# A recurrent memory transformer's forward step, joined differently: V's projection behind the scores, heads paired by parity, V's rows moved by GpSimd, DMA and VectorE

## The chip, the cores and the metric

One Trainium2 chip, one core of it. The time is the device time of the whole kernel in microseconds (us); runs of the kernel before lie between 3055.53 and 3083.94, median 3065.29 (3 runs). Profiles are single executions; all durations below are from the profiled execution of the kernel before.

Engines: TensorE (PE; PEld is its weight load), VectorE (DVE), ScalarE (ACT), GpSimd (POOL) and SyncE (SP, which here only issues DMAs). Each engine and each issuing queue works in the order in which its instructions were written.

## The reference

A pre-norm block: attention over segments with a recurrent memory, then a SwiGLU feed-forward, and the gradients of all weights and inputs for a given output gradient. What matters here is the attention, with 2048 tokens of width 448, 16 heads of width 256, 64 segments of 32 tokens and 8 memory rows, so L = 40 rows a segment:

```python
for s in range(n_seg):
    xs = x[:, s * seg_len:(s + 1) * seg_len, :].copy()
    h = jnp.concatenate([mem, xs], axis=1)
    q = jnp.einsum('btd,dhe->bhte', h, Wq)
    k = jnp.einsum('btd,dhe->bhte', h, Wk)
    v = jnp.einsum('btd,dhe->bhte', h, Wv)
    scores = jnp.einsum('bhqe,bhke->bhqk', q, k) * scale
    scores = jnp.where(mask[None, None], scores, -1000000000.0)
    p = _softmax(scores, axis=-1)
    o = jnp.einsum('bhqk,bhke->bhqe', p, v)
    o = jnp.einsum('bhte,hed->btd', o, Wo)
    mem = o[:, :M, :].copy()
    outs.append(o[:, M:, :])
```

The memory of segment s+1 is an output of segment s, so the 64 steps can't overlap except for work on rows that don't depend on the memory. The gradient runs through the same 64 steps backwards.

## The kernel before

Four stages run one after the other: the forward loop over 64 segments (`forward_chain`), the feed-forward with its gradients, the backward loop over 64 segments (`backward_chain`), and the weight gradients. The order of every engine's instructions is that of the source (a manual schedule): nothing is reordered.

*Rows.* A segment has 40 rows: the 8 memory rows and the first 24 tokens (32 rows, "A", that need the memory or stand beside it) and the last 8 tokens ("B"). B rows of four segments are projected together, a tile of four segments ahead, in pieces used as filler in the steps (`b_units`, L530: `u1` 16 matmuls, `u2` and `u3` 8 each; every fourth step `o_units`, L586, instead).

*Projections.* `proj` (L464) makes half the columns of one projection, for four groups of 1024 columns (four heads each): 16 matmuls of 512 columns, group g written to the PSUM rows 32g to 32g+31. So a half has two heads of each group, and token t of group g stands in row 32g+t.

*A forward step* (loop at L671), in the order of TensorE: K both halves, V first half, Q first half, turned half of K (`tr_half`, L474, four transposes), Q second half, turned halves of K and Q, V second half in two pieces around the last turned half of Q, scores in two halves of 16 matmuls (L505), 24 filler matmuls, two and one dummy matmuls of 512 columns (`spin`, L847), the turn of P's first half (8 transposes of 40x40, L761), masks for the next step (L488), the turn of the second half, 8 filler matmuls, PV (32 matmuls of 40 rows by 40 columns, L792), output projection (64 matmuls of 224 columns, L583), two transposes of the summed result (L513). A VectorE sum (L518) writes the memory rows of the next step, and that starts its projections.

*V's rows.* PV needs V with a segment's 40 rows as the contraction: `V_sb`, groups 0 and 1 in rows 0 to 39, groups 2 and 3 in rows 64 to 103. The evacuated projection `Vev` has the groups in rows 32g instead, so V's rows are moved (`v_shift`, L649): four pieces of 32 rows by 512 columns a half. Before, VectorE moves the first half's four pieces ahead of the scores, GpSimd two pieces of the second half, and VectorE the last two after the turned P. The 8 B rows come by four small DMAs on SP (`v_b_rows`, L641) that wait until the step before has used V_sb. SP then also stores V (two DMAs, L777), K (L706) and Q (L719) for the backward loop, and GpSimd's queue stores P (L774).

*Softmax.* On VectorE and ScalarE, in two halves (L738 to L748). P is written as `P_sb[104, 8 heads, 40]`: heads 0 to 7 in rows 0 to 39, heads 8 to 15 in rows 64 to 103. The turned P (`PT`) is copied out of PSUM once by VectorE and once by ScalarE.

*A backward step* (loop in `backward_chain`) projects the output's gradient (L1173), evacuates it (`dOev`), turns it (`doT`, L1179) for the scores' gradient (L1452), and moves its rows into `dO_sb` as V's above: `shift`, with the two pieces (0, 1) of the second half on ScalarE behind its copy of `doT`. It loads P (`load_P`) and turned V (`load_vT`) a step or more ahead.

## Time and profile before

| | us |
|---|---|
| median of 3 runs | 3065.29 |
| the profiled execution's own time | 3067.6 |
| its span (first to last instruction) | 3065.8 |
| first 58.8 of the span | loads and first tile |
| 58.8 to 1038 | forward loop, 64 steps |
| 1038 to 1400 | feed-forward |
| 1400 to 2375 | backward loop, 64 steps |
| 2375 to 3065.8 | weight gradients |
| TensorE busy, forward loop | 928.48 of 979.20 |
| VectorE busy, forward loop | 587.00 of 979.20 |
| ScalarE busy, forward loop | 445.66 of 979.20 |

How to read it: the page gives busy time by engine, the chain of work that ended last, and groups of instructions by line. The chain is followed back from the last instruction, at each step to what released it; "issue" is time in which an engine waited for nothing that the profile shows. A line of the chain has its start, its length, the engine, the tile that it wrote and the source line, often that of a helper: L431 is a VectorE copy and L434 a ScalarE copy of the forward loop, L1164 and L1167 those of the backward loop. A TensorE entry that looks busy may be pipelined. In a line of the timeline the number after the start is the time from the first instruction of a merged group to its last one's end.

### The profile page before, as it was taken

To read this page: it belongs to the slowest core of one execution; us is meant where nothing else is said; L and a number is where in the kernel's file an instruction comes from. 1 tells how busy PE (TensorE), PEld (TensorE's weight loads), DVE (VectorE), ACT (ScalarE), POOL (GpSimd) and SP (SyncE) were. 2 spreads that over 40 slices of the span, in tenths; PEclk is the share of its full clock that TensorE was granted. 3 is DMA by queue.
4 is the path that set the end of the run, shared out by engine and by line. 5 is a ranking of instruction groups with operands and counts; after the bars stand their busy time and mean duration, and the time that the engine had idled before them with its cause. 6 is when DMAs were issued, how large, how long until landed. Compare 5 with 4: busy or idle time off the path is not lost.

```text
span 3065.8 us, 108383 instructions
## 1 busy us (share of the span) xinstructions
PE 2825.9 (92%) x46532; PEld 1540.9 (50%) x46568; DVE 1546.5 (50%) x4123; ACT 1175.4 (38%) x3023; POOL 738.1 (24%) x1384
## 2 busy tenths in 40 slices
PE   3999999999999699995999999999998999989999
PEld 1555555555555355552555555555554454444454
DVE  4566666666655477772655566556554112211221
ACT  2444444444444356562444444444443111101110
POOL 1222222222222122221222222223222222223332
PEclk7999999999999899997999999999999999999999
DMA  8333333333333773348566566555566999999996
GB/s 262 101 103 114 114 104 108 119 104 105 107 119 99 200 181 116 117 133 188 138 183 154 143 177 158 143 169 171 138 158 197 309 222 197 197 204 208 195 208 135
DMA packets 612448, 482.84 MB, mean 157 GB/s; under 512 B 482944, under 2 KB 526544, under 8 KB 602432
## 3 DMA queue, kind: packets, MB, share of 16 engines
q1 hardware_dynamic: 565632, 289.17, 43.6%
q0 software_dynamic: 46336, 186.74, 18.3%
q8 instruction: 366, 6.00, 0.8%
q14 instruction: 114, 0.93, 0.1%
HBM read 135.08 MB, written 219.52 MB: 116 GB/s over the span
## 4 chain that ended last, share of the span: by engine, by line
PE 75%; issue 6%; DMA 5%; DVE 5%; ACT 5%; SPq 2%; POOL 1%; POOLq 0%; ACTq 0%; DVEq 0%
PE psf L468 14%; PE psf L1669 12%; PE psf L1200 10%; PE psf L1173 4%; PE psf L583 4%; PE psf L1474 3%; PE psf L1654 3%; PE psf L978 3%; PE psh L474 3%; ACT dO_sb L1167 2%; PE psf L1682 2%; PE psf L1061 2%; DMA wall<-in_A_Wv_dram 2%; PE s_ps L847 1%; PE pob L1200 1%
## 5 line engine op out<-in xcount | busy, mean ns | idle before, releaser
L468 PE MATMUL psf<-wall,hA 112*32 112x512 bf16 x6144 | 379.3, 381 | 17.0 <-DVE hA L518 15.2
L1669 PE MATMUL psf<-wall,H_all 128*128 128x512 bf16 x1404 | 320.9, 381 | 13.1 <-DMA wall<-dKA 11.0
L1669 PEld LDWEIGHTS <-H_all 128*128 128x128 bf16 x1440 | 139.5, 98 | 178.2 <-issue 21.2
L468 PEld LDWEIGHTS <-hA 112*32 112x32 bf16 x6144 | 140.5, 96 | 163.8 <-DVE hA L518 31.3
L1581 DVE CAST resc<-psf 128x512 bf16<-128x512 f32 (+1 forms) x58 | 39.1, 673 | 317.4 <-PE psf L1669 283.3
L731 POOL COPY V_sb<-Vev 32x512 bf16<-32x512 bf16 x128 | 77.6, 606 | 341.0 <-PE s_ps L505 329.9
L1579 ACT CAST resc<-psf 128x512 bf16<-128x512 f32 (+1 forms) x54 | 31.0, 574 | 329.0 <-PE psf L1669 291.6
L1525 POOL COPY dmem<-dA 128x32 bf16<-128x32 bf16 x63 | 13.3, 211 | 553.8 <-DVE dA L1212 553.8
L468 PE MATMUL psf<-wall,hB 112*32 112x512 bf16 x1536 | 105.6, 397 | 32.8 <-DMA wall<-in_A_Wk_dram 13.4
L1164 DVE COPY partC<-psf 128x224 f32<-128x224 f32 x64 | 25.1, 392 | 219.6 <-ACT partC L1167 219.6
L1173 PE MATMUL psf<-wall,dA 128*32 128x512 bf16 x2048 | 123.4, 383 | 13.0 <-DVE dA L1212 13.0
L1654 PEld LDWEIGHTS <-wall 128*128 128x128 bf16 x864 | 84.3, 99 | 90.4 <-issue 12.6
L1654 PE MATMUL psf<-dOut_all,wall 128*128 128x448 bf16 x640 | 125.7, 355 | 3.3 <-DMA wall<-OTA 3.3
L583 PE MATMUL psf<-wall,oA 128*32 128x224 bf16 x4096 | 115.5, 268 | 11.8 <-DVE oA L431 11.6
L1200 PE MATMUL psf<-wall,dkA 128*32 128x448 bf16 x2048 | 112.0, 361 | 14.3 <-DMA wall<-in_A_Wk_dram 13.0
L1164 DVE COPY dO_sb<-dOev 32x512 bf16<-32x512 bf16 x256 | 121.0, 472 | 7.1
L1200 PE MATMUL psf<-wall,dqA 128*32 128x448 bf16 x2048 | 111.1, 357 | 13.0 <-DMA wall<-in_A_Wq_dram 10.0
L1200 PE MATMUL psf<-wall,dvA 128*32 128x448 bf16 x2048 | 121.8, 357 | 0.7 <-issue 0.7
L431 DVE COPY V_sb<-Vev 32x512 bf16<-32x512 bf16 x384 | 109.4, 285 | 9.2
L1167 ACT CAST dOev<-psf 128x512 bf16<-128x512 f32 x64 | 37.5, 586 | 184.7 <-PE psf L1173 180.9
L583 PEld LDWEIGHTS <-oA 128*32 128x32 bf16 x4096 | 97.3, 99 | 19.7 <-DVE oA L431 18.4
L1200 PE MATMUL pob<-wall 128*32 128x448 bf16 x1536 | 106.4, 356 | 0.3 <-issue 0.3
(281 smaller groups left out, 5736.2 us busy)
## 6 DMA issues: line engine op xcount, KB each, us to landing
Vtok<-V_sb SPq DMA_DIRECT2D x128, 192.0 KB
KtokA<-Kev SPq DMA_DIRECT2D x64, 256.0 KB
QtokA<-Qev SPq DMA_DIRECT2D x64, 256.0 KB
OTA<-oA POOLq DMA_DIRECT2D x16, 1024.0 KB
Q_sb<-QtokA SPq DMA_DIRECT2D x128, 128.0 KB
K_sb<-KtokA SPq DMA_DIRECT2D x128, 128.0 KB
dVA<-dvA POOLq DMA_DIRECT2D x16, 1024.0 KB
dKA<-dkA POOLq DMA_DIRECT2D x16, 1024.0 KB
```

The lines of the kernel that those rows point to most:

```text
L431: nc.vector.tensor_copy(out=out, in_=in_)
L468: nc.tensor.matmul(ps[32 * g:32 * g + 32, :], lhsT=stat(kc), rhs=W_sb[0:DB, kc, c0:c0 + HB], start=(kc == 0), stop=(kc == KC - 1))
L474: nc.tensor.transpose(pt[:, j * P:(j + 1) * P], ev[:, half * HB + j * P:half * HB + (j + 1) * P], ident[:, :])
L583: nc.tensor.matmul(ps[32 * g:32 * g + 32, 0:2 * DB], lhsT=x, rhs=Wo_sb[:, c, a * 2 * DB:(a + 1) * 2 * DB], start=first, stop=last)
L978: nc.tensor.matmul(out[b][:, 0:BW], lhsT=xT[:, kc, :], rhs=Wx[:, kc, f0:f0 + BW], start=(kc == 0), stop=False)
L1164: nc.vector.tensor_copy(out=out, in_=in_)
L1167: nc.scalar.copy(out=out, in_=in_)
L1173: nc.tensor.matmul(ps[32 * g:32 * g + 32, :], lhsT=stat(kc), rhs=WoT_sb[:, kc, c0:c0 + HB], start=(kc == 0), stop=(kc == KC - 1))
L1200: nc.tensor.matmul(pO[32 * g:32 * g + 32, 0:D], lhsT=ch(c), rhs=WT[:, c, :], start=(first and i < 4), stop=(last and i >= MC - 4), skip_gr ...
L1474: nc.tensor.matmul(po[:, n * L:(n + 1) * L], lhsT=lhs[b:b + L, lc:lc + P], rhs=rhs[b:b + L, hh, :], start=True, stop=True)
L1654: nc.tensor.matmul(ps[:, 0:D], lhsT=stat[:, i, c * P:(c + 1) * P], rhs=Y[:, i, 0:D], start=(i == 0), stop=(i == kts - 1))
L1669: nc.tensor.matmul(ps[:, 0:N], lhsT=Hx[:, i, dc * P:(dc + 1) * P], rhs=X[:, i, b * N:(b + 1) * N], start=(i == 0), stop=(i == kts - 1))
```

## The change

In the forward step, the order of TensorE is now: K, Q (both halves each), four turned halves, V first half, scores, V second half, then 16 filler matmuls, the masks, the turns of P with 8 filler matmuls between, PV's first half, 8 filler matmuls, PV's second half. The dummy matmuls are gone.

V is projected by parity of the head (`proj_v`): even heads to rows 0 to 63, odd heads to rows 64 to 127 of the result, so after the row move V_sb has even heads in rows 0 to 39 and odd heads in rows 64 to 103. P is written with 64 columns a head, so that a block of 128 columns holds two heads; one transpose of 104x104 turns four heads' P. The turned P is copied, one copy for each half and parity, into a tile that is zero but for the two diagonal blocks, and one matmul of 104 rows by 80 columns makes PV of two heads. The four copies: three on ScalarE, one on VectorE.

V's row moves: of the first half two by GpSimd, two by DMA on SP; of the second half two by DMA on SP, two by VectorE behind the softmax. K's and Q's stores move on SP behind V's moves. kT and qT have one buffer instead of two. P goes through HBM with 64 columns a head instead of 40; the backward loop reads it so, and picks V's chunks in the new order. In the backward step one of ScalarE's two moves of dO's rows stands ahead of its copy of the turned half.

The diff, cut to its core:

```diff
+    def proj_v(ps, stat, half, kcs=range(4)):
+        for kc in kcs:
+            wv = Wv_sb[0:DB, kc, :].rearrange("p (x y f e d) -> p x y f e d", x=2, y=2, f=2, e=2)
+            for g in range(G):
+                e, x = divmod(g, 2)
+                nc.tensor.matmul(ps[32 * g:32 * g + 32, :].rearrange("t (y d) -> t y d", y=2), lhsT=stat(kc),
+                                 rhs=wv[:, x, :, half, e, :], start=(kc == 0), stop=(kc == KC - 1))
...
+    def D_(out, in_):
+        nc.sync.dma_start(out=out, in_=in_)
...
-        nc.sync.dma_start(out=dr["KtokA"][s], in_=Kev[:])
-        pv0 = ps1()
-        proj(pv0, Wv_sb, stat, 0)
-        A(Vev[:, 0:HB], pv0[:, :])
...
-        A(fm_view(kT, 0, 0, SEG), tr_half(Kev, 0))
-        v_shift(V_sb, Vev, 0, (0, 1), V)
...
-        V(fm_view(kT, 1, 0, SEG), tr_half(Kev, 1))
-        nc.sync.dma_start(out=dr["QtokA"][s], in_=Qev[:])
+        V(fm_view(kT, 0, 0, SEG), tr_half(Kev, 0))
+        A(fm_view(kT, 1, 0, SEG), tr_half(Kev, 1))
         V(fm_view(qT, 0, 0, SEG), tr_half(Qev, 0))
-        v_shift(V_sb, Vev, 0, (2, 3), V)
+        V(fm_view(qT, 1, 0, SEG), tr_half(Qev, 1))
...
-        pv1 = ps1()
-        proj(pv1, Wv_sb, stat, 1, range(0, 2))
-        A(fm_view(qT, 1, 0, SEG), tr_half(Qev, 1))
-        proj(pv1, Wv_sb, stat, 1, range(2, 4))
+        pv0 = ps1()
+        proj_v(pv0, stat, 0)
+        A(Vev[:, 0:HB], pv0[:, :])
+        v_shift(V_sb, Vev, 0, (0, 1), G_)
+        v_shift(V_sb, Vev, 0, (2, 3), D_)
         scores(qT, kT, 0)
         scores(qT, kT, 1)
-        A(Vev[:, HB:GF], pv1[:, :])
-        v_shift(V_sb, Vev, 1, (0, 1), lambda out, in_: nc.gpsimd.tensor_copy(out=out, in_=in_))
+        pv1 = ps1()
+        proj_v(pv1, stat, 1)
...
             nc.scalar.activation(out=E_sb[0:NR, half], in_=S_sb[half][0:NR], func=ACT.Exp, scale=k.scale)
+        A(Vev[:, HB:GF], pv1[:, :])
+        v_shift(V_sb, Vev, 1, (0, 1), D_)
+        nc.sync.dma_start(out=dr["KtokA"][s], in_=Kev[:])
+        nc.sync.dma_start(out=dr["QtokA"][s], in_=Qev[:])
...
+        v_shift(V_sb, Vev, 1, (2, 3), V)
         cur["u1"]()
         cur["e1"]()
-        cur["u2"]()
-        PT = work.tile([P, HG, L], BF16, name="PT", bufs=2)
+        PT = PTs[s % 2]
...
+            for i in range(2):
+                nc.tensor.transpose(ppt[half][:, i * P:i * P + NR], P_sb[0:NR, 2 * i + half, :], ident[0:NR, 0:NR])
+
+        def p_ev(half, e, eng):
+            eng(PT[QB * e:QB * e + L, half, :, e * L:(e + 1) * L].rearrange("p (g a) n -> p g a n", g=2),
+                ppt[half][QB * e:QB * e + L, 0:2 * P].rearrange("p (a g n) -> p g a n", a=2, g=2)[:, :, :, 0:L])
+
         if s + 1 < NSEG:
             mask_mm(0)
             mask_mm(1)
+        p_turn(0)
+        p_ev(0, 0, A)
+        p_ev(0, 1, A)
+        cur["u2"]()
         p_turn(1)
-        cur["u3"]()
-        for gg, eng in ((0, V), (1, A)):
-            b = QB * gg
-            eng(PT[b:b + L], ppt[gg][b:b + L, 0:HG * L].rearrange("p (h n) -> p h n", n=L))
-        v_shift(V_sb, Vev, 1, (2, 3), V)
+        p_ev(1, 0, A)
+        p_ev(1, 1, V)
...
         for half in range(2):
+            if half == 1:
+                cur["u3"]()
             for gg in range(2):
...
+                pw = po[:, 0:8 * L].rearrange("p (a e c n) -> p a e c n", a=2, e=2, c=DC)
+                for i in range(2):
+                    for dc in range(DC):
+                        c0 = gg * GF + half * HB + i * Dh + dc * P
+                        nc.tensor.matmul(pw[:, i, :, dc, :], lhsT=V_sb[0:NR, c0:c0 + P],
+                                         rhs=PT[0:NR, half, 2 * gg + i, :].rearrange("p (e n) -> p e n", e=2),
+                                         start=True, stop=True)
...
         t1 = tr_half(dOev, 1)
+        shift(1, (0,), A)
         A(fm_view(doT, 1, 0, SEG), t1)
-        shift(1, (0, 1), A)
+        shift(1, (1,), A)
```

More of the change, by code (lines that the diff above doesn't have):

```diff
@@ L261, in run_all @@
     doutTd = dram.tile([NT, P, KC * P], BF16, name="doutTd")
-    P_all = dram.tile([NSEG, 64 + L, H // 2 * L], BF16, name="P_all")
+    P_all = dram.tile([NSEG, 64 + L, H // 2 * 64], BF16, name="P_all")
     dr = dict(XN=XN, Hh=Hh, HN=HN, DH=DH, Zt=Zt, DGP=DGP, DU=DU, QtokA=QtokA, KtokA=KtokA, QtokB=QtokB, KtokB=KtokB, Vtok=Vtok,
@@ L434, in A, with G_ @@
         nc.scalar.copy(out=out, in_=in_)
+    def G_(out, in_):
+        nc.gpsimd.tensor_copy(out=out, in_=in_)
     def slot(s):
@@ L494, in hsel @@
     def hsel(x, half):
-        return x[0:NR].rearrange("p (a b i) n -> p a b i n", a=2, b=2)[:, :, half, :, :]
+        return x[0:NR].rearrange("p (a b) (i n) -> p a b i n", b=2, i=2)[:, :, half, :, 0:L]
     def hview(x):
@@ L536, in stat, with mm @@
             return T.hB[0:DB, kc, :, :]
+        def mm(ps, half, kcs=range(4)):
+            if which == "v":
+                proj_v(ps, stat, half, kcs)
+            else:
+                proj(ps, W_sb, stat, half, kcs)
         def u1():
             st["p0"] = ps1(FP32)
-            proj(st["p0"], W_sb, stat, 0)
+            mm(st["p0"], 0)
         def e1():
@@ L548, in u2 @@
             st["p1"] = ps1(FP32)
-            proj(st["p1"], W_sb, stat, 1, range(0, 2))
+            mm(st["p1"], 1, range(0, 2))
         def u3():
-            proj(st["p1"], W_sb, stat, 1, range(2, 4))
+            mm(st["p1"], 1, range(2, 4))
         def e3():
@@ L665, in forward_chain @@
     nc.gpsimd.memset(V_sb[:], 0.0)
+    Ps, PTs = [], []
+    for i in range(2):
+        Ps.append(work.tile([P, HG // 2, P], BF16, name=f"P_sb{i}", bufs=1))
+        nc.gpsimd.memset(Ps[i][:], 0.0)
+        PTs.append(work.tile([P, 2, 4, 2 * L], BF16, name=f"PT{i}", bufs=1))
+        nc.gpsimd.memset(PTs[i][:], 0.0)
     mask_mm(0)
@@ L690, in forward_chain @@
         late2["et"]()
-        kT = work.tile([P, MC, L], BF16, name="kT", bufs=2)
-        qT = work.tile([P, MC, L], BF16, name="qT", bufs=2)
+        kT = work.tile([P, MC, L], BF16, name="kT", bufs=1)
+        qT = work.tile([P, MC, L], BF16, name="qT", bufs=1)
         nc.gpsimd.tensor_copy(out=kT[:, :, SEG:L], in_=T.kB[:, :, r * M:(r + 1) * M])
@@ L717, in forward_chain @@
         A(Qev[:, HB:GF], pq1[:, :])
-        V(fm_view(kT, 1, 0, SEG), tr_half(Kev, 1))
-        nc.sync.dma_start(out=dr["QtokA"][s], in_=Qev[:])
+        V(fm_view(kT, 0, 0, SEG), tr_half(Kev, 0))
+        A(fm_view(kT, 1, 0, SEG), tr_half(Kev, 1))
         V(fm_view(qT, 0, 0, SEG), tr_half(Qev, 0))
-        v_shift(V_sb, Vev, 0, (2, 3), V)
+        V(fm_view(qT, 1, 0, SEG), tr_half(Qev, 1))
         if s == NSEG - 1:
             ff.load_first()
-        pv1 = ps1()
-        proj(pv1, Wv_sb, stat, 1, range(0, 2))
-        A(fm_view(qT, 1, 0, SEG), tr_half(Qev, 1))
-        proj(pv1, Wv_sb, stat, 1, range(2, 4))
+        pv0 = ps1()
[3 more added lines that the diff above has]
+        v_shift(V_sb, Vev, 0, (2, 3), D_)
         scores(qT, kT, 0)
         scores(qT, kT, 1)
-        A(Vev[:, HB:GF], pv1[:, :])
-        v_shift(V_sb, Vev, 1, (0, 1), lambda out, in_: nc.gpsimd.tensor_copy(out=out, in_=in_))
+        pv1 = ps1()
+        proj_v(pv1, stat, 1)
         mx, ssum, rs, S_sb = [], [], [], []
         E_sb = work.tile([P, 2, HQ, L], FP32, name="E_sb", bufs=1)
-        P_sb = work.tile([P, HG, L], BF16, name="P_sb", bufs=2)
+        P_sb = Ps[s % 2]
         for half in range(2):
@@ L749, in forward_chain @@
                                     in1=hview(rs[half][0:NR].unsqueeze(2).to_broadcast([NR, HQ, L])), op=ALU.mult)
+        v_shift(V_sb, Vev, 1, (2, 3), V)
         cur["u1"]()
         cur["e1"]()
-        cur["u2"]()
-        PT = work.tile([P, HG, L], BF16, name="PT", bufs=2)
+        PT = PTs[s % 2]
         ppt = [ps1(BF16), ps1(BF16)]
         def p_turn(half):
-            for gg in range(2):
-                b = QB * gg
-                for hh in range(HG):
-                    if (hh // 2) % 2 == half:
-                        nc.tensor.transpose(ppt[gg][b:b + L, hh * L:(hh + 1) * L], P_sb[b:b + L, hh, :], ident[b:b + L, b:b + L])
-        spin(k, S_ps[0], 2)
-        p_turn(0)
-        spin(k, S_ps[1], 1)
+            for i in range(2):
[3 more added lines that the diff above has]
+                ppt[half][QB * e:QB * e + L, 0:2 * P].rearrange("p (a g n) -> p g a n", a=2, g=2)[:, :, :, 0:L])
         if s + 1 < NSEG:
@@ L767, in forward_chain @@
             mask_mm(1)
+        p_turn(0)
+        p_ev(0, 0, A)
+        p_ev(0, 1, A)
+        cur["u2"]()
         p_turn(1)
-        cur["u3"]()
-        for gg, eng in ((0, V), (1, A)):
-            b = QB * gg
-            eng(PT[b:b + L], ppt[gg][b:b + L, 0:HG * L].rearrange("p (h n) -> p h n", n=L))
-        v_shift(V_sb, Vev, 1, (2, 3), V)
+        p_ev(1, 0, A)
+        p_ev(1, 1, V)
         nc.gpsimd.dma_start(out=dr["P_all"][s], in_=P_sb[0:NR].rearrange("p h n -> p (h n)"))
@@ L782, in forward_chain @@
         for half in range(2):
+            if half == 1:
+                cur["u3"]()
             for gg in range(2):
-                b = QB * gg
                 po = ps1()
-                i = 0
-                for g in (2 * gg, 2 * gg + 1):
-                    for j in range(4 * half, 4 * half + 4):
-                        c = g * NJ + j
-                        hh = c // DC - HG * gg
-                        lc = c * P - gg * 2 * GF
-                        nc.tensor.matmul(po[:, i * L:(i + 1) * L], lhsT=V_sb[b:b + L, lc:lc + P], rhs=PT[b:b + L, hh, :],
+                pw = po[:, 0:8 * L].rearrange("p (a e c n) -> p a e c n", a=2, e=2, c=DC)
+                for i in range(2):
+                    for dc in range(DC):
+                        c0 = gg * GF + half * HB + i * Dh + dc * P
+                        nc.tensor.matmul(pw[:, i, :, dc, :], lhsT=V_sb[0:NR, c0:c0 + P],
+                                         rhs=PT[0:NR, half, 2 * gg + i, :].rearrange("p (e n) -> p e n", e=2),
                                          start=True, stop=True)
-                        i += 1
                 pov = po[:, 0:8 * L].rearrange("p (g j n) -> p g j n", g=2, j=4)
@@ L841, in forward_chain @@
     out_ev(NT - 1)
-def spin(k, ps, n, reps=4):
-    x = k.ident[:, :].unsqueeze(1).to_broadcast([P, reps, P])
-    for _ in range(n):
-        k.nc.tensor.matmul(ps[:, 0:reps * P], lhsT=k.ident[:, :], rhs=x, start=True, stop=True, skip_group_check=True)
 def _get_small(k):
@@ L1319, in load_P @@
     def load_P(s):
-        p = work.tile([P, HG, L], BF16, name="P_b", bufs=2)
+        p = work.tile([P, HG, QB], BF16, name="P_b", bufs=2)
         nc.gpsimd.dma_start(out=p[0:NR].rearrange("p h n -> p (h n)"), in_=dr["P_all"][s])
@@ L1451, in backward_chain @@
                     c = h * DC + dc
+                    cv = (h % 2) * (MC // 2) + gg * NJ + ((h // 2) % 2) * 4 + ((h // 4) % 2) * 2 + dc
                     nc.tensor.matmul(S_ps[QB * gg:QB * gg + L, hh * L:(hh + 1) * L], lhsT=doT[:, c, :],
-                                     rhs=vT[:, c, 0:L],
+                                     rhs=vT[:, cv, 0:L],
                                      start=(half == 0 and hh == 0 and dc == 0), stop=(dc == DC - 1), skip_group_check=True)
         prod = work.tile([P, HG, L], FP32, name="prod", bufs=1)
-        nc.vector.tensor_tensor(out=prod[0:NR], in0=dP_v, in1=P_sb[0:NR], op=ALU.mult)
+        nc.vector.tensor_tensor(out=prod[0:NR], in0=dP_v, in1=P_sb[0:NR, :, 0:L], op=ALU.mult)
         rsum = smal.tile([P, HG], FP32, name="rsum")
@@ L1461, in backward_chain @@
         dS = work.tile([P, HG, L], BF16, name="dS", bufs=1)
-        nc.vector.scalar_tensor_tensor(out=dS[0:NR], in0=prod[0:NR], scalar=k.scale, in1=P_sb[0:NR], op0=ALU.mult, op1=ALU.mult)
+        nc.vector.scalar_tensor_tensor(out=dS[0:NR], in0=prod[0:NR], scalar=k.scale, in1=P_sb[0:NR, :, 0:L], op0=ALU.mult, op1=ALU.mult)
         def outer(lhs, rhs, dstA, dstB, engs, pairs=False):
@@ L1473, in outer @@
                         lc = c * P - gg * 2 * GF
-                        nc.tensor.matmul(po[:, n * L:(n + 1) * L], lhsT=lhs[b:b + L, lc:lc + P], rhs=rhs[b:b + L, hh, :],
+                        nc.tensor.matmul(po[:, n * L:(n + 1) * L], lhsT=lhs[b:b + L, lc:lc + P], rhs=rhs[b:b + L, hh, 0:L],
                                          start=True, stop=True)
@@ L1550, in backward_chain @@
         nc.tensor.transpose(pm[0:M, c0:c0 + P], dmem0T[:, kc, :], ident[:, :])
-    dmf = work.tile([P, D], BF16, name="dm0", bufs=1)
+    dmf = work.tile([P, D], BF16, name="dm0", tag="dOev", bufs=1)
     dm = dmf[0:M, :]
```

## The prediction

> **What bounds the kernel now.** I read the page's list of engines first, then the chain of work that ended last, first whole and then inside one step of each of the two recurrent loops, and last the timeline of the single engines and of the DMA queue in that same step.

> ```profile
> span 3065.8 us, 108383 instructions
> PE 2825.9 (92%) x46532; PEld 1540.9 (50%) x46568; DVE 1546.5 (50%) x4123; ACT 1175.4 (38%) x3023; POOL 738.1 (24%) x1384
> ```

> 92% looks like a kernel bound by TensorE, but the page's list warns that pipelined matmuls look busy. In the chain the forward loop's first 64 matmuls recur every 15.05 us (498.61, 513.66, 528.71 and so on), whatever kind of step it is: 64 equal steps. So I cost one step and multiply. One step of the chain, from its first score to the next step's first projection (start, length, what):

> ```profile
> 505.53 0.68 PE s_ps L505 x29
> 506.20 1.41 PE psf L468 x24
> 507.61 0.54 PE s_ps L847 x2
> 508.15 0.25 PE psh L761 x8
> 508.40 0.32 PE s_ps L847
> 508.72 0.25 PE s_ps L488 x4
> 508.97 0.23 PE psh L761 x8
> 509.20 0.02 issue
> 509.23 0.32 DVE PT L431
> 509.55 0.03 issue
> 509.58 0.28 DVE V_sb L431
> 509.86 0.03 issue
> 509.89 0.29 DVE V_sb L431
> 510.18 0.03 issue
> 510.21 0.44 DVE oA L431
> 510.65 0.04 issue
> 510.69 1.75 PE psf L583 x64
> ```

> TensorE is the path up to the last turned P (509.20), with filler (L468, the spins of L847). Then VectorE is: one copy of P, two V row moves queued ahead of the copy of the attention's result, and only then the output projection L583. In the backward loop, the same view shows ScalarE where V's counterpart is moved:

> ```profile
> 1809.06 0.59 ACT doT L1167
> 1809.67 0.62 ACT dO_sb L1167
> 1810.31 0.63 ACT dO_sb L1167
> 1810.98 0.38 PE psf L1474 x12
> ```

> The timeline of the DMA queue gives the prices of SP's issues: 192 KB of V stored (two issues of 0.336 each, the second at 510.20), and four small SBUF to SBUF moves of V's memory rows, about 0.63 each:

> ```profile
> 507.52 3.02 SPq L777 DMA_DIRECT2D Vtok<-V_sb  x2
> 510.65 3.41 SPq L646 DMA_DIRECT2D V_sb<-bevv  x4
> ```

> **The change, part by part** (times from a step's first projection; the step above began at 498.61, scores at 6.92, last turned P at 10.59, output projection at 12.08, next step at 15.05).

> *V behind the scores.* Ahead of the scores stand now K and Q (64 matmuls, 3.64 by the chain), 16 transposes (0.33+0.55+0.33 = 1.21) and one V half (0.98): scores at 5.83, 1.09 sooner. Their last operand is VectorE's fourth turned half: its transposes end at 4.85, VectorE copies two halves of 0.42 back to back until 5.44. That is covered by the V half on TensorE; without it the scores would wait 0.6. VectorE no longer moves V rows there.

> *Between scores and turned P.* TensorE: scores 0.67, second V half 0.98, 16 filler matmuls 0.94, mask 0.25; first turn at 8.67. The spins go (0.86). VectorE's softmax starts 0.47 after the scores and gives its halves 2.06 and 2.86 later (row 506.00 to 508.06 and 508.86): 8.36 and 9.16, both before TensorE asks. Two transposes of 128 columns cost 0.16 a half (four cost 0.33, so 82 ns each) against 0.23 to 0.25; with the 8 filler matmuls between (0.55) the last turn ends at 9.54: 1.05 sooner than 10.59.

> *Copies of turned P.* ScalarE has to do, in order, the second exponential (ends 1.64 after the softmax's start, 7.94), V's second half 0.59, the filler's copy 0.57, then three of the four PT copies of 40x160. No row has one; 40x320 took 0.42 and two of 128x64 took 0.33, so 0.17 to 0.42, and between them by width 0.28. The second ends at 9.66, and the first PV matmuls start at 9.70. VectorE's own (fourth) copy waits for ScalarE's third in the built order, until about 10.2; behind it stand the copies of the result, needed at 11.2, so that wait is hidden; longer by 1 us it would not be.

> *PV with two heads in one.* 16 matmuls of 104 rows and 80 columns replace 32 of 40 and 40. The old ones went at 26 ns each (32 in 0.82), the 128-column transposes at 82; 80 columns lie between, I take 60: 0.48 a half. Ends: 0.53 to 1.31 for all, against my 0.96 (33 is 80 columns at the projections' rate of 512 in 228 ns for four). [...] Filler (0.55) now stands between the halves: halves at 9.70 and 10.73, end 11.21. PE's extra semaphore waits on V (up to four a load, 0.05 each by the one such event in the trace) cost 0 to 0.2; I take 0.05, since the first lie in the wait for PT.

> *V rows by three ways.* GpSimd's two moves (1.27 by its row) follow V's first half from 6.4 to 7.7, needed at 9.70: hidden. SP gets four issues more a step. Two follow V's first half at 6.4; two its second half, which ScalarE ends at 8.53. Bounds: an issue of 0.34 (V's store) or 0.63 (the rows nearest in kind, SBUF to SBUF). Stored V's data moved from 0.78 after the issue began and SP could reuse its rows about 0.7 after the data ended (data until 511.95, third move of 510.65's four at about 512.65); the 0.63 kind moved from 1.35 on. With 0.2 for 32 KB: seen 1.7 or 2.25 after the issue. The later two then are in at 10.28 and 10.65, or 10.83 and 11.50, against 10.73 and 10.97 where PV's second half asks: 0 to 0.53 late. Both rows are equally near (one in kind, one in rows), so 0.2. The earlier two are in by 9.3 at the latest. Behind them on SP: stores of K and Q (moved from early in the step to here, read by nobody in this loop; K's buffer is wanted again at about 15.5, its store done by 12), V's stores, which wait until V is whole, about 11.5, then the next step's memory rows, which wait for V's store to be read, 2.45 after its issue: 14.1 to 16.6, 2.2 into the next step. SP's next urgent issue is at 6.4 there and PV at 9.7: hidden, 4 us of cover.

> *Sum, forward.* Output projection at 11.21+0.05+0.2 = 11.46 instead of 12.08; its first half (0.87) covers the copies of PV's second half (0.44); the tail is unchanged. 0.62 a step, times 63: -39. In the last step the feed-forward weights load: there memory rows took 7.92 (1017.60, waited for in the chain), and the second V moves meet that load: +3 (0 to +6).

> *Backward.* ScalarE moves one dO part before the turned half arrives (it idled 0.54 there) instead of after: the last move ends at about 10.42 of 1800 instead of 10.94, doT 0.1 later, which the first half of the scores covers. TensorE comes 0.52 sooner to the turn of dS, at 1812.15, but dS ends at 1812.34 (VectorE, four operations of 0.49 that are not moved): 0.27 of it is kept. In steps whose filler is shorter (0.49) less: 0.25, bounds 0 and 0.3. Times 62: -15.

> *Free:* wider P rows (1024 B for 640, 104 KB for 65 each way) are loaded a step ahead; strided reads of P move the same 320 elements; four memsets on GpSimd before the first step end long before the weights (chain: DMA until 55). If that cover were gone: 2 us, once.

> Total -39+3-15 = -51 against the profiled 3067.6 (span 3065.8): 3016. The median shown is 2.3 lower, less than the runs' own spread, so no correction.

> **The rivals.**

> *A. V's DMA becomes the wait (the slower side).* At PV's second half. Loads in the backward loop took 4.0 to 4.4 in the chain (K_sb, Q_sb). With 4.2 from the later issue (8.9) the rows are in at 13.1, 2.1 late instead of 0.2: a step 1.3 longer than now, +82+3-15: 3137. For: SP's queue serves stores too. Against: K and Q are issued behind, and those slow rows come from HBM. It decides from rows in at 12.0, 3.1 after the issue. 10%.

> *B. TensorE and ScalarE give it back.* PV at 82 ns (+0.35), PT copies 0.42 (+0.28), semaphores (+0.15), less the DMA wait that they hide (-0.2): 0.58 of 0.62 lost. 3067.6-3+3-15 = 3053. For: copies on ScalarE are serial. 13%.

> *C. Backward gains nothing.* VectorE's chain or loads of vT end the wait anyway: 3031 from my forward sum, with a DMA wait of 0.3: 3037. 13%.

> *D. The DMA is hidden whole.* Late 0, PV at 50 ns: 0.2+0.1 better: -0.9 a step, 3067.6-57+3-15 = 2999, 15%.

> *E. The clock.* The spins go. In the stretch from turned P to the next step the granted clock was 1.00 with TensorE busy 3.81 of 4.46:

> ```profile
> 509.20:513.66 4.46, 3.81 (x109) 2.58 (x108) 2.19 (x9) 1.71 (x6) 0.52 (x1) 1.00 0.31 77
> ```

> After it the longest new gap is about 0.5 us. If the clock halved in the 3.6 us of projections, each step would lengthen by 3.6: over 3240. 2%. [...]

> **How the numbers follow.** My forecast 47% (own range 3002 to 3034), D 15, B 13, C 13, A 10, E 2. Predicted 3016. The range 2990 to 3064 takes in D, C and B, and leaves out A, E and a tail of D. 1% is 31 us, about what a measurement of this kernel can tell from no change: faster (below 3035) 0.62 from forecast and D; within 0.26 from B and C; slower 0.12 from A and E.

> **What would show it.** Scores 5.8 after a step's first projection; no idle of TensorE before the turns; first PV matmul at 9.7; its second half waiting for a DMA into V_sb 0 to 0.5; a forward step of 14.4 instead of 15.05; in the backward loop one dO move between the dOev and doT copies of ScalarE and steps about 0.25 shorter. I am wrong if forward steps are longer than 14.8, or if V_sb's DMA is in later than 3 us after its issue.

## The result, and the profile after

| | before | after |
|---|---|---|
| median, us (4 runs each) | 3071.07 | 3035.55 |
| lowest and highest, us | 3055.53, 3083.94 | 3018.21, 3046.04 |
| ratio after/before, 95% interval | | 0.9854 [0.9807, 0.9901] |
| profiled execution's own time, us | 3067.6 | 3044.81 |
| granted clock, whole span | 0.976 | 0.971 |

The ratio is that of the measurement with its interval, not the quotient of the two medians, which is 0.9884 and lies inside the interval. By the ratio the gain is 45 us (1.46% of 3071), by the medians 35.5. The page's head after:

```profile
span 3043.0 us, 105017 instructions
PE 2775.7 (91%) x44548; PEld 1530.2 (50%) x44584; DVE 1501.9 (49%) x3931; ACT 1164.3 (38%) x3087; POOL 737.2 (24%) x1388
```

TensorE has 1984 matmuls fewer and VectorE 192 instructions fewer, yet the busy shares are the same to within a point: the head says nothing of where the time went. For that I took the times of the VectorE sum that ends each step (`hA` in the forward loop, `dA` in the backward one) and formed the 62 differences of each loop:

| | before | after |
|---|---|---|
| first forward step done at, us | 76.5 | 83.4 |
| forward loop, 62 steps: sum, mean, us | 936.3, 15.10 | 891.2, 14.37 |
| backward loop, 62 steps: sum, mean, us | 906.6, 14.62 | 907.1, 14.63 |
| end of the backward loop to the end of the span, us | 719.4 | 732.1 |

The forward loop gives 45.1 us, as much as the ratio says; part of that agreement is chance, as the last step of the loop gives some of it back (below). The two profiled spans differ by only 22.8, mostly since the first stage and the last were 6.9 and 12.7 longer in this execution of after; in the other kernels below, which leave both alone, they vary between 73 and 87 and between 719 and 742. So a change in a loop is read from the loop here, and the time from the ratio.

One forward step in the chain of waits (start, length, what), to be held against that of before:

```profile
500.93 3.64 PE psf L471 x64
504.57 1.13 PE psh L485 x16
505.70 0.98 PE psf L479 x16
506.68 0.44 PE s_ps L516 x19
...
507.15 0.34 DVE mx L759
...
508.70 0.58 ACT Vev L434
...
509.29 0.51 SPq L667
509.80 0.04 issue
509.84 2.74 DMA V_sb<-Vev
...
512.62 0.32 PE psf L816 x4
512.94 1.65 PE psf L600 x64
```

The scores come 5.75 after the step's first projection. The path then leaves TensorE for the softmax, ScalarE's copy of V's second half (508.70), SP's issue of one row move (509.29), and the 2.74 from the start of the next one's issue until its rows have landed; before, it went through TensorE's filler and VectorE's row moves. The timeline of TensorE shows how much of that is a wait (in brackets: idle time before, and its releaser):

```profile
510.12 0.27 PE L783 MATMUL psh<-ident,P_sb 104*128 104x104 bf16 x2
510.36 0.53 PE L816 MATMUL psf<-PT,V_sb 104*128 104x80 bf16 x8
510.83 0.61 PE L471 MATMUL psf<-wall,hB 112*32 112x512 bf16 x8
511.37 0.32 PE L816 MATMUL psf<-PT,V_sb 104*128 104x80 bf16 x4
512.62 0.32 PE L816 MATMUL psf<-PT,V_sb 104*128 104x80 bf16 x4 [0.93 <-DMA V_sb<-Vev]
```

PV's first half and half of its second run without a pause; the last four matmuls wait 0.93 for group 1 of V. Elsewhere in the loop the same move lands after 1.89 or 2.30 (chain of the two steps that follow), and less or nothing is waited for:

```profile
524.74 1.89 DMA V_sb<-Vev
...
539.25 2.30 DMA V_sb<-Vev
```

So the steps are 14.0 to 14.1 where the rows come in time or nearly so (the commonest value), and up to 15.1 where they don't. Three are longer for another reason. The last two of the 62 (16.49 and 15.32) are long as in the kernel before (16.51 and 16.37). One in the middle took 16.36: in it the granted clock was at half from 225.6 to 229.1, behind two waits for these rows, and the output projection took 3.16 instead of 1.72:

```profile
225.33 0.32 PE L816 MATMUL psf<-PT,V_sb 104*128 104x80 bf16 x4 [0.63 <-DMA V_sb<-Vev]
225.57 3.16 PE L600 MATMUL psf<-wall,oA 128*32 128x224 bf16 x64
```

The waits of the forward loop name these rows (engine, line, releaser: us in total, times, longest; a load and its matmul can both be counted for one delay):

```profile
PEld L816 <- DMA V_sb<-Vev: 18.7, 47, 1.3
...
PE psf L816 <- DMA V_sb<-Vev: 14.8, 32, 1.1
```

In the backward loop the chain after passes through VectorE's four operations, no longer through ScalarE's moves of `dO`:

```profile
1819.91 0.74 PE s_ps L1472 x31
...
1820.67 0.50 DVE prod L1476
...
1821.19 0.50 DVE rsum L1478
...
1821.71 0.50 DVE prod L1479
...
1822.24 0.50 DVE dS L1482
1822.74 0.04 issue
1822.79 0.49 PE psh L1521 x16
```

Its steps inside a tile went from 14.30, 14.60, 14.30 to 14.15, 14.40, 14.15. Every fourth step, at a tile's end, took 14.4 to 16.1 before and 14.2 to 20.2 after. The 47 plain steps lost 9.5 us in sum (680.8 to 671.3), the 15 at a tile's end gained 10.0 (225.8 to 235.8). In the longest of these TensorE stood still for 1.33 and 2.12 without anything that the profile shows to wait for, and then had the clock at half for 6.8.

### The profile page after: what moved, and what is told of

Read it like the earlier page. It is cut to its first block, busy times and chain, and to the rows that moved or that the text cites. A ratio compares the mean times of both kernels' runs of the same rounds, so it can differ in the third digit from the quotient of the medians.

```text
span 3043.0 us, 105017 instructions
## 1 busy us (share of the span) xinstructions
PE 2775.7 (91%) x44548; PEld 1530.2 (50%) x44584; DVE 1501.9 (49%) x3931; ACT 1164.3 (38%) x3087; POOL 737.2 (24%) x1388
## 4 chain that ended last, share of the span: by engine, by line
PE 71%; DMA 8%; DVE 7%; issue 6%; SPq 3%; ACT 3%; POOL 1%; another core or an unknown queue 0%; POOLq 0%; ACTq 0%; DVEq 0%
PE psf L1689 12%; PE psf L1218 9%; PE psf L471 9%; PE psf L1191 4%; PE psf L600 4%; DMA V_sb<-Vev 3%; PE psf L479 3%; PE psf L1494 3%; PE psf L1674 3%; PE psf L996 3%; PE psh L485 2%; PE psf L1702 2%; PE psf L1079 2%; DMA wall<-in_A_Wv_dram 2%; PE pob L1218 2%
## 5 line engine op out<-in xcount | busy, mean ns | idle before, releaser
L471 PE MATMUL psf<-wall,hA 112*32 112x512 bf16 x4096 | 233.4, 380 | 17.0 <-DVE hA L529 15.2
L471 PEld LDWEIGHTS <-hA 112*32 112x32 bf16 x4096 | 103.5, 97 | 129.8 <-DVE hA L529 31.3
L479 PE MATMUL psf<-wall,hA 112*32 112x512 bf16 x2048 | 134.0, 382 | 0.0
L1674 PEld LDWEIGHTS <-wall 128*128 128x128 bf16 x864 | 84.5, 99 | 95.9 <-issue 14.3
L1218 PE MATMUL psf<-wall,dkA 128*32 128x448 bf16 x2048 | 113.8, 364 | 18.6 <-DMA wall<-in_A_Wk_dram 13.1
L1218 PE MATMUL psf<-wall,dqA 128*32 128x448 bf16 x2048 | 113.2, 362 | 14.9 <-DMA wall<-in_A_Wq_dram 10.6
L1185 ACT CAST wall<-psf 128x64 bf16<-128x64 f32 x512 | 106.7, 247 | 0.0
L471 PE MATMUL psf<-wall,hB 112*32 112x512 bf16 x1024 | 75.6, 397 | 30.1 <-DMA wall<-in_A_Wk_dram 18.6
```

Source lines behind the costliest of these rows:

```text
L471: nc.tensor.matmul(ps[32 * g:32 * g + 32, :], lhsT=stat(kc), rhs=W_sb[0:DB, kc, c0:c0 + HB], start=(kc == 0), stop=(kc == KC - 1))
L479: nc.tensor.matmul(ps[32 * g:32 * g + 32, :].rearrange("t (y d) -> t y d", y=2), lhsT=stat(kc), rhs=wv[:, x, :, half, e, :], start=(kc == ...
L1185: nc.scalar.copy(out=out, in_=in_)
L1218: nc.tensor.matmul(pO[32 * g:32 * g + 32, 0:D], lhsT=ch(c), rhs=WT[:, c, :], start=(first and i < 4), stop=(last and i >= MC - 4), skip_gr ...
L1674: nc.tensor.matmul(ps[:, 0:D], lhsT=stat[:, i, c * P:(c + 1) * P], rhs=Y[:, i, 0:D], start=(i == 0), stop=(i == kts - 1))
```

## The experiments

All ratios are against the kernel before on the same chip. The first four kernels shared one set of runs of it, the last four another. "Loop" is the sum of the 62 forward steps as above.

**The backward half undone.** Changed kernel, with the old order of `dO` moves.

```
-        shift(1, (0,), A)
         A(fm_view(doT, 1, 0, SEG), t1)
-        shift(1, (1,), A)
+        shift(1, (0, 1), A)
```

> The changed kernel with ScalarE's two dO moves of the backward step put back behind its copy of doT; the forward loop as changed. My theory (the reordering shortens each backward step by 0.15 to 0.2 us, as the plain steps of the two traces do: 14.30 to 14.15, 14.60 to 14.40): plain backward steps go back to 14.30 and 14.60, about +10 us of 3036, forward steps unchanged (median 14.1). Rival (the sums of the two backward loops, 906.6 and 907.1, are equal, so the reordering brings nothing; what the plain steps gain comes from the new layout of P or V's chunks): plain steps stay at 14.15 and 14.40.

Measured 3050.56, ratio 0.988 [0.9845, 0.9916]; loop 891.4 (after 891.2). The backward steps inside a tile went back to 14.29, 14.60, 14.30: the reorder is what shortened them. Its loop's sum is 906.4 against 907.1 with the reorder. The gain of the plain steps, 47 of them by some 0.16, is 8 us; it is inside the spread of the boundary steps and of the ratio, whose interval overlaps that of after. The forward half makes the result.

**V's second half by GpSimd instead of DMA.**

```
-        v_shift(V_sb, Vev, 1, (0, 1), D_)
+        v_shift(V_sb, Vev, 1, (0, 1), G_)
```

> The changed kernel with the second half's two V moves that go by DMA done by GpSimd instead (they would end about 1.3 us after ScalarE's copy, near 9.2 of a step; PV's second half asks at 10.7). My theory (forward steps above 14.0 us wait for these DMA rows): nearly all forward steps at 14.0 to 14.1, mean 14.4 to 14.1, -18 to -22 us against the changed kernel, and no wait of PE for V_sb<-Vev in the second half. Rival (GpSimd's copies slow VectorE's softmax, or its own queue is late with P's store): median step above 14.1. Rival (the long steps come from another wait, such as ScalarE's wait for the memory rows V_sb<-bevv): mean stays at 14.3 or more.

Measured 3013.35, ratio 0.9753 [0.9686, 0.9819], the best of the study; loop 870.3, mean step 14.04, most steps 13.88. The chain of one step:

```profile
504.04 0.20 PE psh L783 x2
504.24 0.55 PE psf L479 x8
504.78 0.25 PE psh L783 x2
505.03 0.48 PE psf L816 x8
505.51 0.55 PE psf L479 x8
506.06 0.41 PE psf L816 x8
506.46 1.70 PE psf L600 x64
```

From the first turn to the output projection TensorE does not pause. The DMA of the second half cost the changed kernel 0.33 a step in the mean (14.37 to 14.04), 20.9 us over the loop: shown, since nothing else differs; some 1.5 us of it is the one step at half clock, which has no counterpart here. What is left above 13.88 is in part the first half's rows, still moved by DMA: TensorE's matmuls waited 4.2 us for them, nine times.

**K's and Q's stores behind V's.** Two candidates for the late rows: the two large stores issued right behind the moves on the same queue hold them up, or the moves are simply that slow.

```
         v_shift(V_sb, Vev, 1, (0, 1), D_)
-        nc.sync.dma_start(out=dr["KtokA"][s], in_=Kev[:])
-        nc.sync.dma_start(out=dr["QtokA"][s], in_=Qev[:])
...
             nc.sync.dma_start(out=dr["Vtok"][s, gg], in_=V_sb[QB * gg:QB * gg + 48, :])
+        nc.sync.dma_start(out=dr["KtokA"][s], in_=Kev[:])
+        nc.sync.dma_start(out=dr["QtokA"][s], in_=Qev[:])
```

> The changed kernel with K's and Q's stores issued behind V's stores instead of right behind the V moves. Theory 1 (the late rows are held up by the 512 KB of stores that follow them on the same DMA engines): the wait for V_sb<-Vev falls from 0.25 us a step to under 0.1, mean step 14.37 to 14.15, -14 us. Theory 2 (the rows are late by their own issue of 0.5 us each and the landing of 1.9 us or more, whatever follows): mean step stays at 14.3 to 14.4, time as the changed kernel within 5 us.

Measured 3044.32, ratio 0.9862 [0.9818, 0.9906]; loop 898.9, mean 14.50; TensorE's matmuls waited 18.0 us for these rows, against 14.8 in the changed kernel and 20.0 in the first experiment, which has the same forward loop. The rows land with the same spread as well: 1.84 to 3.80 from the start of their issue in this kernel's chain, 1.83 to 3.23 in the changed kernel's. So the stores behind the moves are not what delays them. The loop's 14.50 is no clean measure of the moves, for other things changed with it: the copies into `Kev` now wait for K's store (58.2 us in 26 waits on ScalarE, 37.8 in 31 on VectorE), and the clock fell to half in two steps (16.49 and 16.54). Why one move lands after 1.8 and another after 3.2 stays open; the other large transfer at that time, P's store of 104 KB on GpSimd's queue, was moved in no run.

**The joined order with the old heads.** The kernel before with the new order (V behind the scores, rows by GpSimd, DMA and VectorE, K's and Q's stores behind, filler between turns and PV halves, no dummy matmuls), but with P, its turn and PV as they were. Its core:

```
-        v_shift(V_sb, Vev, 0, (2, 3), V)
...
+        pv0 = ps1()
+        proj(pv0, Wv_sb, stat, 0)
+        A(Vev[:, 0:HB], pv0[:, :])
+        v_shift(V_sb, Vev, 0, (0, 1), G_)
+        v_shift(V_sb, Vev, 0, (2, 3), D_)
         scores(qT, kT, 0)
...
-        spin(k, S_ps[0], 2)
-        p_turn(0)
-        spin(k, S_ps[1], 1)
```

> The kernel before with the joined order alone: V's first half ahead of and its second half behind the scores, V moved by GpSimd, DMA and VectorE, K's and Q's stores behind, no dummy matmuls, masks ahead of P's turn, filler between; but heads, P's turn (16 small transposes), two PT copies and 32 small PV matmuls as before, and the backward step as before. If the order is what shortens the step: 14.3 to 14.5, -35 to -45 us against before; if the pairing of heads (8 small turns and 16 PV matmuls saved, copies in parts) carries as much: 14.7 or more, -20 us.

Measured 3135.04, ratio 1.0165 [1.0112, 1.0218]: slower than before. Loop 965.2; steps mostly of two kinds, 14.5 to 14.9 and 16.0 to 16.4. Granted clock of the forward loop 0.94 (1.00 before and after). In one long step, per microsecond (busy time of PE, PEld, DVE, ACT, POOL, then the granted clock):

```profile
521.00:522.00 1.00, 0.38 (x13) 0.41 (x14) 0.44 (x2) 0.35 (x1) 0.36 (x1) 1.00 0.25 66
522.00:523.00 1.00, 1.00 (x20) 0.40 (x18) 0.42 (x1) 0.37 (x1) 0.00 (x0) 0.76 0.96 310
523.00:524.00 1.00, 1.00 (x32) 0.88 (x34) 0.65 (x3) 0.50 (x3) 0.00 (x0) 0.50 1.15 348
524.00:525.00 1.00, 1.00 (x28) 0.88 (x24) 0.04 (x1) 0.11 (x1) 0.00 (x0) 0.50 0.82 191
525.00:526.00 1.00, 1.00 (x32) 0.88 (x28) 0.00 (x0) 0.00 (x0) 0.00 (x0) 0.54 0.37 135
526.00:527.00 1.00, 0.85 (x20) 0.42 (x8) 0.00 (x0) 0.35 (x1) 0.00 (x0) 1.00 0.02 8
```

The timeline of TensorE there; the first line is from the step before, where the clock held:

```profile
508.46 1.72 PE L589 MATMUL psf<-wall,oA 128*32 128x224 bf16 x64
...
521.62 0.63 PE L796 MATMUL psf<-PT,V_sb 40*128 40x40 bf16 x16 [0.78 <-DVE PT L431]
...
523.39 2.93 PE L589 MATMUL psf<-wall,oA 128*32 128x224 bf16 x64
```

A rest of 0.78 before PV, in a stretch of short 40-row matmuls, and the clock is at half from about 522.5 to 525.9: the output projection takes 2.93 instead of 1.72. The step before had a rest of 0.68 at the same place and kept its clock. This was my rival E, in a kernel I had not meant it for. Two more runs separate the clock from the order.

**The same with three dummy matmuls behind the last turn**, and **the kernel before without its dummies**:

```
         p_turn(1)
+        dm = ps1()
+        spin(k, dm, 3)
```

> The joined order with the old heads, and three dummy matmuls of 128x512 behind the last turn of P, where TensorE rested 0.7 to 0.8 us in each step of that kernel; their result is read by nobody. Theory (what made that kernel slow is the granted clock, which fell to 0.50 after this rest in the steps of 16.1 us, and not the order or the old heads' work): the clock of the forward loop is back at 1.00, nearly all steps at 14.5 to 14.7, -30 to -40 us against before. Rival (the steps are long for another cause and the clock only follows): steps stay bimodal at 14.6 and 16.1, 1 to 2% slower than before.

```
-        spin(k, S_ps[0], 2)
         p_turn(0)
-        spin(k, S_ps[1], 1)
```

> The kernel before without its three dummy matmuls a step, nothing else. Theory (without them TensorE rests some 1.2 us a step around P's turn, and the granted clock falls in some steps, as with the joined order and the old heads): forward clock 0.93 to 0.97, steps of 15.0 and 16.5 mixed, +20 to +50 us. Rival (the dummies only fill a wait; the clock stays): all steps at 15.0, within 5 us of before.

With the dummies the joined order has its clock back (1.00) and takes 3076.43, ratio 0.9991 [0.9956, 1.0026]; loop 923.7, mean 14.90: 0.20 a step better than before, a smaller gain than the expected step of 14.5 to 14.7, and the expected 30 to 40 us can't be seen in the time. Without its dummies the kernel before falls to 0.93 in the loop and takes 3127.45, ratio 1.0161 [1.0104, 1.0219]; steps of 15.05 and 16.5 mixed. In one of the long ones TensorE rests 0.65, 0.39 and 0.15 within little more than three microseconds, and the clock is at half from about 518.1 to 521.5 (0.55 and 0.74 in the microseconds at the edges, 0.50 between):

```profile
515.94 0.22 PE L761 MATMUL psh<-ident,P_sb 40*40 40x40 bf16 x3 [0.65 <-DVE P_sb L748]
...
516.74 0.28 PE L761 MATMUL psh<-ident,P_sb 40*40 40x40 bf16 x8 [0.39 <-DVE P_sb L748]
...
518.51 1.50 PE L583 MATMUL psf<-wall,oA 128*32 128x224 bf16 x28 [0.15 <-DVE oA L431]
```

So the dummies were worth 1.6% in the kernel before. It is the paired heads that let the changed kernel do without them: without dummies the clock falls in about half of the steps with the old heads, in the old order and in the new one, against one step in the changed kernel and none in the next one. (The last two steps are left out of this count; the clock falls there in the kernel before as well, at 991.9 and 1009.0, in steps of 16.51 and 16.37.)

**The paired heads with the old order ahead of the scores**: changed kernel, but V, its row moves (VectorE, VectorE, GpSimd, VectorE) and the stores of K and Q where they were before.

```
-        v_shift(V_sb, Vev, 0, (0, 1), G_)
-        v_shift(V_sb, Vev, 0, (2, 3), D_)
         scores(qT, kT, 0)
         scores(qT, kT, 1)
-        pv1 = ps1()
-        proj_v(pv1, stat, 1)
+        A(Vev[:, HB:GF], pv1[:, :])
+        v_shift(V_sb, Vev, 1, (0, 1), lambda out, in_: nc.gpsimd.tensor_copy(out=out, in_=in_))
```

> The pairing alone: V projected by parity, P with 64 columns a head, two turns a half, four copies, 16 PV matmuls of 104 rows, no dummies, filler between and VectorE's last V moves behind the softmax as in the changed kernel, but K, V, Q, V and the turned halves ahead of the scores in the old order, V moved by VectorE, VectorE, GpSimd and VectorE, K's and Q's stores early. Theory (the step is TensorE's work in order; behind the scores the softmax leaves TensorE waiting, since only 16 filler matmuls and the masks stand there): scores at 6.9, last turn at about 10.3, PV half an us later, 14.8 to 15.0 a step, -5 to -15 us. If the clock needs the work behind the scores: steps of 15 and 16.4, slower than before.

Measured 3053.68, ratio 0.9928 [0.9894, 0.9961]; loop 916.1, uniform steps of 14.74, clock 1.00. So in the mean step: pairing alone, without the dummies, takes 0.32 off (15.10 to 14.78), the order alone, with dummies, 0.20 (14.90), both 0.73 (14.37). The two help each other: the order without the pairing needs the dummies, and the pairing without the order starts its scores at 6.92 as before.

**All V rows by GpSimd and VectorE, none by DMA** (second experiment, and the first half's pieces as well):

```
-        v_shift(V_sb, Vev, 0, (2, 3), D_)
+        v_shift(V_sb, Vev, 0, (2, 3), G_)
```

> As the kernel with the second half's two DMA moves on GpSimd, and the first half's two DMA moves on GpSimd as well: six moves of 0.6 us on GpSimd, none by DMA. Theory (what is left above 13.88 us a step is the wait for the first half's DMA rows, 9 us in 10 steps): mean step 14.04 to 13.9, -5 to -9 us against that kernel. Rival (GpSimd's last move now ends near 10.3 of a step and slows VectorE's own moves from 0.60 to 0.92, so PV's second half waits for them): mean 14.1 or more, not faster than that kernel.

Measured 3045.29, ratio 0.9891 [0.9831, 0.995]; loop 904.4, uniform steps of 14.52, worse than with the first half by DMA (14.04). GpSimd moves six pieces in 4.04 and VectorE's own two run beside it; one of the softmax's two products on VectorE (`P_sb`) takes 0.72 there instead of 0.33. VectorE's copies into `V_sb`, first in the changed kernel, then here (count: ns least, median, most):

```profile
L431 DVE COPY V_sb<-Vev x120: 283/288/290, 107.2 to 952.5; 32x512 bf16<-32x512 bf16 x120
```

```profile
L431 DVE COPY V_sb<-Vev x118: 582/607/633, 107.8 to 951.5; 32x512 bf16<-32x512 bf16 x118
```

The copies of turned P, queued behind them on VectorE, come late, and TensorE waits for VectorE and for GpSimd in each step:

```profile
PEld L816 <- POOL V_sb L437: 21.5, 59, 0.4
...
PE psf L816 <- DVE PT L431: 20.3, 59, 0.4
```

So of the mixes that were run, DMA for the early pieces and GpSimd for the late ones is the best.

## Why the prediction was right, and where its terms were off

Predicted were 3016 us from 3067.6, a factor of 0.983; measured is 0.9854 [0.9807, 0.9901], and the median 3035.55 lies in the range, though just above the forecast's own 3002 to 3034. The mechanism in the forward loop was as forecast: TensorE reaches its scores and the last turned P sooner, and PV's second half waits for rows by DMA. The sum came out right in part by luck, by more than one pair of errors that cancel.

*Scores, turns, copies.* Scores 5.83 after the first projection: 5.75. Last turn's end 9.54: 9.46 (510.12 + 0.27 - 500.93). A copy of turned P 0.28 by width: three in 0.98 with their overlap, about 0.3 each. First PV 9.70: 9.43, as ScalarE began those copies 0.3 earlier than I had counted. PV 0.48 a half: 0.47 from the first half's start to the filler's. In the second experiment's chain the two halves take 0.48 and 0.41. A single load of `V_sb` takes 0.096 (median of the 960 between 100 and 960 us after), so sixteen end to end would be 1.54; the sixteen pairs of load and matmul take 0.89, so loads overlap. (The lower bound of 0.53 for PV should have been 0.57 by its own rate: 64 projection matmuls of 512 columns in 3.64 us, so four in 228 ns, and 80 columns of that for each of 16.) Without a wait for rows the step is 14.00 to 14.06, against 14.18 by my terms (14.43 less the 0.2 for rows and 0.05 for semaphores).

*The DMA of V's rows.* Taken as 0.2 late, between 0 and 0.53; it is 0.33 in the mean (the second half's, by the second experiment). The issue took 0.51 to 0.59 in the median of each of the four moves, between my bounds of 0.34 and 0.63; a move landed 1.83 to 3.23 after the start of its issue, where each of my bounds had a single value (1.7 and 2.25). These two errors, 0.15 better and 0.13 worse, cancel: mean step 14.37, and I had 14.4. Two things were missing. The first half's rows were put at nothing ("in by 9.3 at the latest"), and they too are waited for: 4.2 us in nine waits of the second experiment, where no other row comes by DMA, and the commonest step there is 13.88. In the changed kernel 4 of the 38 moves that the chain passes through are of the first half. And of the signs of being wrong that the prediction names, both came true in some steps, though not in the mean: two of these moves land later than 3 us (3.14 and 3.23, both of the first half), and 14 of the 62 steps are longer than 14.8.

*The last step.* +3, between 0 and +6. After, its rows land only 9.40 after the start of their issue:

```profile
974.63 0.23 DVE hA L529
...
983.81 9.40 DMA V_sb<-Vev
...
993.26 0.45 PE psf L816 x4
993.71 3.14 PE psf L600 x64
```

From the sum to the output projection that is 19.08, against 13.26 before (1012.81 to 1026.07): +5.8, at the upper bound. With no V rows by DMA it is 11.83 (last experiment, 987.92 to 999.75). It is one step of 64.

*Backward.* The step that failed. I had -0.25 a step over 62 steps, -15. The plain steps gained 0.15 and 0.20, since VectorE's chain is next, as the prediction said; but the steps at a tile's end, one in four, vary between executions by more than the gain (225.8, 235.8 and 230.1 in sum before, after and with the reorder undone). The sum moved by +0.5 in the profiles, and the time with and without the reorder can't be told apart. Rival C was right in this: the mis-sized term is the -15, which was a price for steps of one kind taken times all steps. Forward, -39 + 3 = -36 by the prediction, gave 45.1 in 62 steps and 5.8 back in the last: -39.3.

*The clock.* Rival E was held at 2%, on the reason that the longest new gap would be about 0.5. In the changed kernel the clock stayed at 1.00 through nearly all of the forward loop, even behind a rest of 0.93 for the DMA, and fell once (225.6 to 229.1, rests of 0.22 and 0.63), which cost some 1.5 us. So the rival's mechanism is there, in one step of 62. The reason against it was too weak: in two kernels with old heads the clock fell to half in every other step, after rests of 0.65 to 0.78, and stayed there for about 3.4 (522.5 to 525.9, 518.1 to 521.5). The length of a rest doesn't decide it, for rests of 0.68 and of 0.93 passed without harm.

*The other rivals.* A, the rows as the new bound, is there in small: they do end many steps, late by 0.33 in the mean instead of the 2.1 that it needed. B's prices (PV at 82 ns, copies at 0.42) are refuted by the lines above. D is what the second experiment makes of the kernel: with the late rows on GpSimd the step is 0.33 shorter, and the ratio is 0.9753.

## What to carry to other kernels

Cost a loop step by step, with one price for each kind of step: a gain in three steps of four is no gain in the sum if the fourth waits for something else and varies by more. A short transfer between two engines' work on the critical path cost 1.83 to 3.23 us here from the start of its issue, besides the issues queued ahead of it; a copy on an idle engine of known length (GpSimd, 0.61) was better there, with a step of 14.04 instead of 14.37, and the transfer belongs where there is slack, as long as few of VectorE's own copies run beside it (in the second experiment half of its copies into `V_sb` took 0.61 instead of 0.29, and it was still the fastest). Before dummy matmuls are taken out, look at what they fill: here they were worth 1.6%, and went without that loss only together with larger matmuls in that stretch (PV of 104 rows by 80 columns instead of 40 by 40).

## What the runs showed of the hardware that I had not expected

- The granted clock halves after rests well under a microsecond, in steps of 15 us with TensorE busy nine tenths of the time (0.93 and 0.91 of the stretch from 100 to 940 us): 0.78 in one kernel, 0.65, 0.39 and 0.15 close together in another. What goes with it, by the fit above, is the work of the matmuls in one window of 3.413 us, not the rest alone. The clock came back about 3.4 us later, after 1.2 us lost on the output projection alone (2.93 instead of 1.72).
- A VectorE copy of 32x512 bf16 takes 0.29 alone and 0.61 beside GpSimd copies of the same shape. GpSimd's own take 0.61 alone; of the six, the one that meets VectorE's first copy takes 0.72 and the one beside its second 0.60. GpSimd's copies began first; VectorE loses about 0.32 a copy and ends each some 0.14 after the GpSimd copy beside it, and GpSimd loses 0.11 in one copy of six. Why the two slow each other isn't shown.
- A 32 KB move within SBUF cost 0.51 to 0.59 of SP's time for its issue, in the median of each of the four, and landed 1.83 to 3.23 after the issue began (17 of 38 moves in the chain of the changed kernel within 1.90), in steps that look alike. Two large stores issued behind it don't account for the spread.
